# Weight transfers gated behind the first q and k, preparation split, its early squares moved to ScalarE, its steps spread over slots, in a fused attention and feed-forward kernel

## The chip, the cores and the metric

One core of a Trainium2 chip. The metric is device time in microseconds (us). Times of a kernel are the median of its executions; most agree within 1%. A profile is one execution, with positions counted from the start of its span, which is about 2 us shorter than the time that the run reports.

PE is the engine of matmuls, DVE is VectorE, ACT is ScalarE, POOL is GpSimd, SP is the engine that issues the loads of q and k.

## The reference

```python
def _attn_ref(q, k, v, g_q, g_k):          # q, k, v: (8, 12, 448, 64)
    q_n, k_n = rmsnorm(q, g_q), rmsnorm(k, g_k)
    scores = (1 / sqrt(64)) * q_n @ k_n^T
    attn = softmax(scores)
    return attn @ v

x = attn_out as (3584, 768)
out = ((x @ w1) * (x @ w2)) @ w3 @ w_out   # d_ff = 1024
```

## The kernel before

The 96 heads are worked on in 24 "quads" of four heads, three quads to a batch. A quad takes four slots. In each slot PE makes scores for two of the quad's eight score tiles (`sc`), ACT takes their exp into `P`, and PE multiplies the last quad's `P` with v (`pv`). Before that, a quad has to be prepared: squares of q and k, their sums (`ssq`), `alpha` = 1/rms by ln and exp on ACT, scaling on DVE (`qtmp`, `qks`), and a transpose into `qkT`, on PE for quads 0 to 3. As w3 and w_out are constants, their product `w34s` is made once: eight steps "fc" of one transpose of w3 (`w3T`) and two groups of matmuls (`wps`). When a batch is done, its feed-forward pieces (`pa`, `pb`, `po`) become fillers, two to a slot.

Parts that the change and the argument touch (shortened; `...` marks cuts):

```python
def prep_sq(i, pr, on_act=False):
    ...
    for t, src in enumerate((s["q"], s["k"])):
        if on_act:
            nc.scalar.activation(out=sq[:, t], in_=src[:, hs], func=AF.Square)
        else:
            nc.gpsimd.tensor_tensor(out=sq[:, t], in0=src[:, hs], in1=src[:, hs], op=MULT)
    nc.vector.tensor_reduce(out=s["ssq"][:, :, hs, :], in_=sq, axis=AX, op=ADD)

def prep_alpha(i):
    ...
    nc.scalar.activation(out=lnv, in_=s["ssq"], func=AF.Ln, bias=eps_t)
    nc.scalar.activation(out=s["alpha"], in_=lnv, func=AF.Exp, scale=-0.5)

# start
load_qk(0, split=2); load_qk(1); load_qk(2)      # issued by SP
load_v(0); 4 x load_wout; make_identity; 4 x load_w3   # issued by POOL
...
# slots
for i in range(NQ + 1):
    ...                       # preps: quad i+1 (i < 3) and quad i+2 (i >= 2)
    for sl in range(4):
        if i < NQ: qk_exp(i, sl)
        if i > 0 and sl < 3: pv_set(i - 1, sl)
        ...
        for n in preps:
            if sl < 2:
                prep_sq(n, sl)
                if sl == 1: prep_alpha(n)
        ...                   # two weight transfers issued
        ...                   # one fc of w34 from slot 6 on, or two fillers
        for n in preps:
            if sl >= 2:
                prep_scale(n, sl - 2, pe=n < 4)
                if n < 4: prep_pe_transpose(n, sl - 2)
```

Each engine works through its instructions in the order in which they are written here.

## Time and profile before

Time before: 431.25 us (median of 4; 430.7 to 432.7). The profile, by stages: up to the first scores, from there to the first w3 transpose, to the first `pa`, to the end.

The windows view of the kernel before: after the stretch and its length comes each engine's busy time with the number of its instructions, then the granted TensorE clock, the DMA engines' share and GB/s.

```profile
0.00:21.70 21.70, 2.13 (x16) 1.27 (x16) 7.16 (x13) 4.35 (x7) 8.37 (x17) 1.00 0.96 195
21.70:45.90 24.20, 12.87 (x93) 4.75 (x92) 14.69 (x14) 11.69 (x16) 16.72 (x24) 1.00 1.15 242
45.90:99.80 53.90, 42.86 (x357) 22.44 (x354) 35.89 (x57) 18.97 (x30) 19.34 (x22) 0.91 0.49 95
99.80:430.70 330.90, 324.11 (x2552) 148.48 (x2548) 227.50 (x313) 199.19 (x305) 95.79 (x88) 1.00 0.59 120
```

PE is the bound only in the last stretch (324.1 of 330.9 us busy, with the end of the last output in it). The first three stretches are 99.8 us in which PE has 57.9 us of work; the room for a gain lies there.

In the middle, two VectorE multiplies collide with GpSimd squares. The timeline of the kernel before; columns: start, duration, engine, line, operation, out<-in, shapes.

```profile
...
32.79 2.70 DVE L158 TENSOR_TENSOR qtmp<-q_sb,alpha 112x512 bf16<-112x512 f32 x1
...
32.89 1.05 POOL L139 TENSOR_TENSOR sq<-q_sb 112x512 f32<-112x512 f32 x1
33.89 1.04 POOL L139 TENSOR_TENSOR sq<-k_sb 112x512 f32<-112x512 f32 x1
...
35.87 2.85 DVE L171 TENSOR_TENSOR qks<-k_sb,alpha 112x512 bf16<-112x512 f32 x1
...
36.11 1.05 POOL L139 TENSOR_TENSOR sq<-q_sb 112x512 f32<-112x512 f32 x1
37.11 1.04 POOL L139 TENSOR_TENSOR sq<-k_sb 112x512 f32<-112x512 f32 x1
```

The `qtmp` multiply took 2.70 us and the `qks` from `k_sb` 2.85 us, each while two squares ran on GpSimd; undisturbed both take 0.69 us.

### The profile page before, as it was taken

The page shows a single profiled execution, that of the slowest core. Times are in us where ns is not written, and L with a number is a line of the kernel's source. Part 1 is how long each engine was busy: PE and PEld are TensorE (multiplying, and loading weights), DVE is VectorE, ACT ScalarE, POOL GpSimd, SP SyncE. Part 2 cuts the span into 40 slices and gives each one's busy share as a digit, 9 for nine tenths or more (in the row PEclk, how much of TensorE's full clock was granted, in tenths as well). Part 3 has the DMA queues.
Part 4 walks back from the last instruction along what each step waited for, and adds up shares of the span by engine and source line. Part 5 has one row for each costly group of instructions (what it writes and reads, how often), then busy time and mean ns, then how long its engine had stood idle before and what let it go on. Part 6 is the DMA issues. An engine that isn't in the chain of part 4 may idle for free.

```text
span 430.7 us, 7455 instructions
## 1 busy us (share of the span) xinstructions
PE 382.0 (89%) x3008; PEld 176.9 (41%) x3008; DVE 285.2 (66%) x396; ACT 234.2 (54%) x357; POOL 140.2 (33%) x150
## 2 busy tenths in 40 slices
PE   0145688789999999999999999999999999999995
PEld 0111344444444444444444444444444454445552
DVE  1547666676677877977888779777987795233232
ACT  2154344146675766566757665766576657662210
POOL 6177618004412531542355324531452350000000
PEclk9999989889999999999999999999999999999999
DMA  7999944242477579587765677679766764103004
GB/s 148 240 250 234 215 107 66 44 104 47 108 149 145 139 128 139 120 191 151 135 140 152 136 150 143 156 148 143 134 156 129 149 126 111 23 0 111 2 8 138
DMA packets 79362, 55.07 MB, mean 128 GB/s; under 512 B 39904, under 2 KB 73184, under 8 KB 79328
## 3 DMA queue, kind: packets, MB, share of 16 engines
q1 hardware_dynamic: 64160, 42.27, 42.0%
q0 software_dynamic: 15168, 12.32, 20.1%
q8 instruction: 23, 0.38, 0.3%
q14 instruction: 11, 0.09, 0.1%
HBM read 46.72 MB, written 11.01 MB: 134 GB/s over the span
## 4 chain that ended last, share of the span: by engine, by line
PE 81%; DVE 8%; DMA 4%; ACT 2%; issue 1%; POOL 1%; SPq 1%; DVEq 0%
PE pa L279 18%; PE pb L296 17%; PE po L318 16%; PE pv L229 13%; PE sc L205 10%; PE wps L265 5%; DMA k_sb<-in_k_dram 4%; DVE qtmp L158 2%; DVE ssq L142 2%; ACT P L214 2%; DVE qks L171 2%; DVE qks L165 1%; POOL sq L139 1%; SPq L92 1%; PE w3T_ps L257 1%
## 5 line engine op out<-in xcount | busy, mean ns | idle before, releaser
L214 ACT ACTIVATE P<-sc 112x896 bf16<-112x896 f32 x192 | 165.3, 913 | 110.2 <-PE sc L205 110.2
L139 POOL TENSOR_TENSOR sq<-q_sb 112x512 f32<-112x512 f32 x46 | 53.9, 1171 | 192.5 <-DMA q_sb<-in_q_dram 172.9
L279 PE MATMUL pa<-xT,w1s 128*128 128x448 bf16 x384 | 83.7, 354 | 0.0
L296 PE MATMUL pb<-xT,w2s 128*128 128x448 bf16 x384 | 83.1, 353 | 0.0
L303 DVE TENSOR_TENSOR abT<-pb,a_sb 128x448 bf16<-128x448 f32 x64 | 39.7, 621 | 63.5 <-PE pb L296 45.0
L318 PE MATMUL po<-w34s,abT 128*128 128x384 bf16 x448 | 77.1, 327 | 0.5 <-DVE o_sb L325 0.4
L142 DVE TENSOR_REDUCE ssq<-sq 112x16 f32<-112x1024 f32 x48 | 57.9, 1211 | 11.8 <-ACT sq L137 7.5
L205 PE MATMUL sc<-qkT 64*112 64x448 bf16 x384 | 60.6, 388 | 2.8 <-ACT P L214 2.8
L139 POOL TENSOR_TENSOR sq<-k_sb 112x512 f32<-112x512 f32 x46 | 54.5, 1186 | 7.6 <-DMA k_sb<-in_k_dram 7.3
L318 PEld LDWEIGHTS <-abT 128*128 128x128 bf16 x448 | 42.1, 98 | 35.1 <-issue 9.1
L296 PEld LDWEIGHTS <-w2s 128*128 128x128 bf16 x384 | 37.6, 98 | 35.1
L279 PEld LDWEIGHTS <-w1s 128*128 128x128 bf16 x384 | 32.9, 98 | 45.4 <-issue 20.7
L171 DVE TENSOR_TENSOR qks<-k_sb,alpha 112x512 bf16<-112x512 f32 x48 | 49.3, 1027 | 0.0
L287 ACT CAST a_sb<-pa 128x448 bf16<-128x448 f32 x64 | 33.6, 525 | 22.3 <-PE pa L279 22.3
L229 PE MATMUL pv<-P,v_sb 112*32 112x448 bf16 x768 | 45.3, 357 | 0.0
L325 DVE COPY o_sb<-po 128x384 f32<-128x384 f32 x56 | 30.1, 552 | 22.4 <-PE po L318 22.4
L158 DVE TENSOR_TENSOR qtmp<-q_sb,alpha 112x512 bf16<-112x512 f32 x48 | 42.3, 881 | 1.3 <-ACT alpha L149 1.3
L245 DVE TENSOR_TENSOR xT<-pv,r 128x448 bf16<-128x448 f32 x48 | 29.9, 622 | 18.3 <-PE pv L229 17.6
L190 PE MATMUL qkT_ps<-ident,qks 112*128 112x112 bf16 x64 | 7.6, 259 | 37.9 <-DVE qks L165 34.6
L205 PEld LDWEIGHTS <-qkT 64*112 64x112 bf16 x384 | 18.5, 129 | 37.8 <-issue 36.8
L165 DVE TENSOR_TENSOR qks<-qtmp,g_b 112x512 bf16<-112x512 bf16 x48 | 31.9, 665 | 1.6
L265 PE MATMUL wps<-w_outs,w3T 128*128 128x384 bf16 x128 | 25.1, 352 | 2.5 <-DVE w3T L260 2.5
(32 smaller groups left out, 175.0 us busy)
## 6 DMA issues: line engine op xcount, KB each, us to landing
q_sb<-in_q_dram SPq DMA_DIRECT2D x23, 448.0 KB, 5.8
k_sb<-in_k_dram SPq DMA_DIRECT2D x23, 448.0 KB, 6.2
v_sb<-in_v_dram POOLq DMA_DIRECT2D x24, 224.0 KB, 4.5
out_dram<-o_sb SPq DMA_DIRECT2D x8, 336.0 KB, 2.8
out_dram<-o_sb SPq DMA_DIRECT2D x8, 288.0 KB, 4.2
w3s<-in_moe_w_dram POOLq DMA_DIRECT2D x8, 256.0 KB, 11.8
out_dram<-o_sb SPq DMA_DIRECT2D x8, 240.0 KB, 4.4
w_outs<-in_moe_w_out_dram POOLq DMA_DIRECT2D x4, 384.0 KB, 11.8
```

Source lines behind the costliest of these rows:

```text
L139: nc.gpsimd.tensor_tensor(out=sq[:, t], in0=src[:, hs], in1=src[:, hs], op=MULT)
L142: nc.vector.tensor_reduce(out=s["ssq"][:, :, hs, :], in_=sq, axis=AX, op=ADD)
L158: nc.vector.tensor_tensor(out=qtmp.transpose([0, 2, 1, 3]), in0=s["q"][:, hs], in1=alpha[:, 0, hs].unsqueeze(3).broadcast_to([NP, 2, J, D] ...
L171: nc.vector.tensor_tensor(out=qks[:, 1].transpose([0, 2, 1, 3]), in0=s["k"][:, hs], in1=alpha[:, 1, hs].unsqueeze(3).broadcast_to([NP, 2, ...
L205: nc.tensor.matmul(out=sc[:, u, 0:S], lhsT=qkT[u * D : (u + 1) * D, pr, J + jk, :], rhs=qkT[u * D : (u + 1) * D, pr, 0:J, :].rearrange("d ...
L214: nc.scalar.activation(out=P[:, 2 * pr : 2 * pr + 2, jk, :], in_=sc[:, :, 0:S], func=AF.Exp)
L229: nc.tensor.matmul(out=ps[h * HALF : (h + 1) * HALF, :], lhsT=w, rhs=P[:, h, jk, :], start=(jk == 0), stop=(jk == J - 1), tile_position=(0 ...
L265: nc.tensor.matmul(out=ps[:, 0:NH], lhsT=w3T[:, gc, fc * 128 : (fc + 1) * 128], rhs=w_outs[:, gc, nh * NH : (nh + 1) * NH], start=(gc == 0 ...
L279: nc.tensor.matmul(out=ps[:, 0:S], lhsT=w1s[:, c, fi * 128 : (fi + 1) * 128], rhs=xT[b][:, c, :], start=(c == 0), stop=(c == CM - 1),)
L296: nc.tensor.matmul(out=ps[:, 0:S], lhsT=w2s[:, c, fi * 128 : (fi + 1) * 128], rhs=xT[b][:, c, :], start=(c == 0), stop=(c == CM - 1),)
L303: nc.vector.tensor_tensor(out=abT[bp][:, fi, odd * S : (odd + 1) * S], in0=ps[:, 0:S], in1=a_tiles.pop((b, fi)), op=MULT,)
L318: nc.tensor.matmul(out=ps[:, 0:NH], lhsT=abT[bp][:, fi, t * 128 : (t + 1) * 128], rhs=w34s[:, fi, nh * NH : (nh + 1) * NH], start=(fi == 0 ...
```

## The change

Its intent: let the first q and k have the DMA engines for themselves, by a copy on GpSimd that waits for the last k of quad 0 ahead of all weight issues (the "gate"); prepare quad 0 pair by pair; square on ScalarE for quads 0 to 3, so that GpSimd only issues transfers early on; spread the preparation of quads 1 to 4 evenly over slots 0 to 11, and put PE's transposes one slot after their scaling.

```diff
+        make_identity(nc, ident)
+        nc.gpsimd.tensor_copy(out=gate, in_=st[0]["k"][:, HQ - 1, 0, 0:1])
         load_v(0)
         ...
-        prep_sq(0, 0, on_act=True)
-        prep_sq(0, 1, on_act=True)
-        prep_alpha(0)
-        prep_scale(0, 0, pe=True)
-        ...
+        for pr in range(2):
+            prep_sq(0, pr, on_act=True)
+            prep_alpha(0, 2 * pr, 2 * pr + 2)
+            prep_scale(0, pr, pe=True)
+            prep_pe_transpose(0, pr)
 ...
+    def prep_step(step):
+        n, part = divmod(step, 4)
+        if part < 2:
+            prep_sq(n, part, on_act=n < N_PE_T)          # N_PE_T = 4
+            if part == 1:
+                prep_alpha(n)
+        else:
+            prep_scale(n, part - 2, pe=n < N_PE_T)
 ...                                                     # in a slot t:
                 if i < NQ:
                     qk_exp(i, sl)
                 if i > 0 and sl < 3:
                     pv_set(i - 1, sl)
+                for fn in pe_t:                          # transposes of the slot before
+                    fn()
-                for n in preps: ...                      # squares, alpha
-                for _ in range(2):
+                for _ in range(4):
                     if wq:
                         wq.pop(0)()                      # weight transfers
+                if t in W34_SLOTS: ...                   # about one fc a slot, t = 5 to 14
+                elif not w34q:
                     fill(2)
-                for n in preps: ...                      # scaling, transposes
+                goal = 4 + ((t + 1) * 16 + 11) // 12 if t < 12 else 20 + t - 11
+                while steps_done < min(goal, 4 * NQ):
+                    prep_step(steps_done)
+                    ...                                  # transposes go to pe_t
+                    steps_done += 1
```

More of the change, by code (lines that the diff above doesn't have):

```diff
@@ L74 @@
     ones = const.tile([NP, HALF], BF, name="ones")
+    gate = const.tile([NP, 1], FP, name="gate")
     eps_t = const.tile([NP, 1], FP, name="eps_t")
@@ L142, in prep_sq, with prep_alpha @@
         nc.vector.tensor_reduce(out=s["ssq"][:, :, hs, :], in_=sq, axis=AX, op=ADD)
-    def prep_alpha(i):
+    def prep_alpha(i, h0=0, h1=HQ):
         s = st[i]
-        lnv = prep_pool.tile([NP, 2, HQ, J], FP, tag="lnv", name="lnv")
-        nc.scalar.activation(out=lnv, in_=s["ssq"], func=AF.Ln, bias=eps_t)
-        s["alpha"] = prep_pool.tile([NP, 2, HQ, J], FP, tag="alpha", name="alpha")
-        nc.scalar.activation(out=s["alpha"], in_=lnv, func=AF.Exp, scale=-0.5)
+        if h0 == 0:
+            s["lnv"] = prep_pool.tile([NP, 2, HQ, J], FP, tag="lnv", name="lnv")
+            s["alpha"] = prep_pool.tile([NP, 2, HQ, J], FP, tag="alpha", name="alpha")
+        lnv = s["lnv"][:, :, h0:h1]
+        nc.scalar.activation(out=lnv, in_=s["ssq"][:, :, h0:h1], func=AF.Ln, bias=eps_t)
+        nc.scalar.activation(
+            out=s["alpha"][:, :, h0:h1], in_=lnv, func=AF.Exp, scale=-0.5
+        )
     def prep_scale(i, pr, pe=False):
@@ L352, in fill @@
                 fillers.pop(0)()
+    N_PE_T = 4
+    def prep_step(step):
[6 more added lines that the diff above has]
+            prep_scale(n, part - 2, pe=n < N_PE_T)
     with tc.manual_schedule():
@@ L363 @@
             load_wout(c)
-        make_identity(nc, ident)
         for c in range(4):
             load_w3(c)
+        load_v(1)
         nc.vector.memset(eps_t, 64e-6)
@@ L372 @@
         )
-        prep_sq(0, 0, on_act=True)
-        prep_sq(0, 1, on_act=True)
-        prep_alpha(0)
-        prep_scale(0, 0, pe=True)
-        prep_pe_transpose(0, 0)
-        prep_scale(0, 1, pe=True)
-        prep_pe_transpose(0, 1)
+        for pr in range(2):
[3 more added lines that the diff above has]
+            prep_pe_transpose(0, pr)
         wq = [lambda c=c: load_w3(c) for c in range(4, CF)]
+        wq.append(lambda: load_v(2))
         for h in range(HQ):
@@ L387 @@
                     )
-        W34_FROM = (1, 2)
-        fc_next = [0]
+        wq.append(lambda: load_v(3))
+        w34q = [lambda: w3_transpose(0)]
+        for fc in range(CF):
+            if fc + 1 < CF:
+                w34q.append(lambda fc=fc: w3_transpose(fc + 1))
+            for nh in range(2):
+                w34q.append(lambda fc=fc, nh=nh: w34_unit(fc, nh))
+        W34_SLOTS = {5: 4, 6: 3, 7: 3, 8: 3, 9: 3, 10: 3, 11: 2, 12: 2, 13: 2, 14: 2}
+        steps_done = 4
+        pe_t = []
         for i in range(NQ + 1):
@@ L394 @@
                 load_qk(i + 3)
-            preps = []
-            if i < 3:
-                preps.append(i + 1)
-            if 2 <= i and i + 2 < NQ:
-                preps.append(i + 2)
             for sl in range(4):
+                t = 4 * i + sl
                 if i < NQ:
@@ L404 @@
                     pv_set(i - 1, sl)
-                if sl == 0 and i + 1 < NQ:
+                if sl == 0 and 4 <= i + 1 < NQ:
                     load_v(i + 1)
-                for n in preps:
-                    if sl < 2:
-                        prep_sq(n, sl)
-                        if sl == 1:
-                            prep_alpha(n)
-                for _ in range(2):
+                for fn in pe_t:
+                    fn()
+                pe_t = []
+                for _ in range(4):
                     if wq:
                         wq.pop(0)()
-                if (i, sl) >= W34_FROM and fc_next[0] < CF:
-                    fc = fc_next[0]
-                    if fc == 0:
-                        w3_transpose(0)
-                    if fc + 1 < CF:
-                        w3_transpose(fc + 1)
-                    w34_unit(fc, 0)
-                    w34_unit(fc, 1)
-                    fc_next[0] += 1
-                else:
-                    fill(2)
-                for n in preps:
-                    if sl >= 2:
-                        pe = n < 4
-                        prep_scale(n, sl - 2, pe=pe)
-                        if pe:
-                            prep_pe_transpose(n, sl - 2)
+                if t in W34_SLOTS:
+                    for _ in range(W34_SLOTS[t]):
+                        if w34q:
+                            w34q.pop(0)()
+                elif not w34q:
+                    fill(2)
+                goal = 4 + ((t + 1) * 16 + 11) // 12 if t < 12 else 20 + t - 11
+                while steps_done < min(goal, 4 * NQ):
+                    n, part = divmod(steps_done, 4)
+                    prep_step(steps_done)
+                    if part >= 2 and n < N_PE_T:
+                        pe_t.append(lambda n=n, pr=part - 2: prep_pe_transpose(n, pr))
+                    steps_done += 1
         fill(len(fillers))
```

## The prediction

> **What bounds the kernel now.** From 99.86 us on (first pa matmul) PE is the bound: the windows view gives it 313.4 of 315.1 us busy. Before, it is not: empty until 17.5 us, busy 12.9 of 24.2 us from 21.7 to 45.9 us, and 42.9 of 54.0 us from there to 99.9. The prize lies in the first 100 us. Causes, from the chain of waits and the timeline:
>
> 1. The first q and k share the DMA engines with v, w_out and w3. The four first loads (0.9 MB) land at 6.4, 8.5, 11.2 and 13.8 us while 2.4 MB moves; squares and alpha for all four heads precede any scaling; first scores 21.7 us. k of quad 1 lands at 23.7 us.
> 2. GpSimd squares (1.04 us a half, ScalarE 0.63) stand between its weight issues. While they run, two VectorE multiplies take 2.70 and 2.85 us instead of 0.69. The Trainium skill (SBUF — State Buffer, Who interferes with whom) says that a VectorE instruction with two SBUF inputs contends with a GpSimd one that reads SBUF; this trace agrees.
> 3. PE transposes stand right behind their VectorE scaling: PE waits 7.7 us for qks from 40 to 99.8 us. Some w34 groups run cold: 16 wps matmuls take 4.34 us at 81.3 us, 2.76 at 74.9 (granted clock 0.73 for 80 to 90 us). The skill (TensorE: Matmul & The Clock Gate, What's actually happening) blames idleness; the trace shows slow groups behind PE gaps, not the mechanism.
>
> **What the change does.** No PE work is removed. The gate moves weight transfers behind k of quad 0. ScalarE gains 12 squares (7.6 us), GpSimd loses them (12.5 us). The first alpha is split. Transposes go one slot behind their scaling. Preps of quads 1 to 4 spread over 12 slots; w3/w_out work starts one slot earlier at about one fc per slot.
>
> **On the path.** At the 240 GB/s seen with both queues, 1.1 MB alone should be in by about 9 us instead of 13.8; the last half's square, reduce, ln/exp, three multiplies and transposes cost about 5 us (estimate from the durations): first scores near 14.5 us, 7 earlier. k of quad 1 lands about 15 to 17 us. Slots 0 to 4 are then bound by ScalarE (1.7 us of exp a slot plus squares): the first w3 transpose moves from 45.9 to about 29 us. Weights do not decide: 12 MB at 240 GB/s is done by about 55 us, w3's first chunk by about 27. From there to the fillers warm PE work is about 40 us (8 × 3.2 w34, scores 5, pv 7, transposes 3), VectorE work about as much; with a quarter for waits 51 us instead of 54, but one slot further. First pa near 78 us instead of 99.9, with one slot (1.4 us) less left. PE's remaining 313 us and the 16 us end stay. Sum: 431.5 − 22 − 1.4 ≈ 408 us.
>
> **Right or wrong will show as:** k of quad 0 in before 10 us; first scores 13 to 16 us; k of quad 1 before 18 us; no early multiply over 1 us before quad 4; PE waits for qks below 2 us between 40 us and first pa; first pa 72 to 84 us; first pa to end within 3 us of 330.
>
> **What would make it wrong.** ScalarE waiting for alpha inside a slot, holding back exp (in-order queues); VectorE, at about PE's load, stalling PE through the two shared mm buffers; weights arriving late, so w34 or first pa waits for DMA; a low granted clock through the denser stretch. Better than predicted if w34 runs at 3.2 us a slot without waits: near 398 us.
>
> Chances: faster 0.96, within 2% 0.03, slower 0.01. Predicted 408 us, range 398 to 417.

## The result, and the profile after

425.2 us (424.95 to 425.86 in the four fast executions of five), against 431.25 us; the ratio is 0.9857, 95% interval 0.983 to 0.9885. Ratios here and below are the mean time of one kernel's fast runs over that of the other's of the same rounds, so not quite the ratio of the medians. The change gains 6 us where 23 were forecast, and the range 398 to 417 us missed.

The fifth, which came first, took 971.9 us. In it groups of six `pa` matmuls took 3.16 us instead of 1.24 from beginning to end, and PE was 98% busy. It is left out of everything below; what caused it was not found. The change's trace is that of a further execution of the same kernel, run for it:

> The changed kernel, unedited. Its first profile fell in an execution of 972 us in which every matmul was about 2.8 times slower, while four other executions took 425 us. If that execution was an accident of the chip and not of the kernel, this one takes 424 to 427 us, with 128x448 matmuls at 0.19 us apart as in the kernel before, and the profile can be compared. My forecast's mechanism then says first pa at 72 to 84 us and 330 us from there to the end. The rival, since only 6 us were gained: the first pa comes near 93 us because the w34 stretch is slower than 51 us. A second rival: the first pa does come near 78 us and the later stretch is longer by some 15 us.

It took 425.85 us. The windows view of the changed kernel, cut at the same events:

```profile
0.00:16.10 16.10, 2.14 (x16) 1.27 (x16) 6.96 (x13) 4.63 (x9) 6.11 (x15) 1.00 0.88 201
16.10:36.70 20.60, 12.44 (x82) 5.27 (x82) 12.07 (x17) 16.16 (x26) 5.78 (x10) 1.00 1.14 235
36.70:90.00 53.30, 43.11 (x371) 23.14 (x368) 39.67 (x57) 21.26 (x33) 19.79 (x27) 0.94 0.72 134
90.00:423.90 333.90, 327.44 (x2546) 150.81 (x2544) 209.78 (x311) 196.92 (x304) 89.64 (x88) 0.99 0.57 119
```

| stage | before | forecast | after | forecast was off by |
|---|---|---|---|---|
| start to first scores | 21.7 | 14.5 | 16.1 | +1.6 |
| to the first w3 transpose | 24.2 | 14.5 | 20.6 | +6.1 |
| to the first `pa` | 53.9 | 49 | 53.3 | +4.3 |
| to the end | 330.9 | 329.5 | 333.9 | +4.4 |
| span | 430.7 | 407.5 | 423.9 | +16.4 |

(The forecast's stages are differences of the positions it names: 14.5, 29 and 78 us, and the last stretch of before less 1.4 us. Its text names 51 us for the third stretch, which its positions do not bear out.) All four terms were too small, and the last stretch even grew. Three places of the changed kernel's timeline say why. First, slot 1, whose exps come late (columns as before; in brackets the idle time of the engine before the line, and what ended it):

```profile
...
19.57 2.35 DVE L143 TENSOR_REDUCE ssq<-sq 112x16 f32<-112x1024 f32 x2 [2.73 <-ACT sq L138]
19.95 0.63 ACT L138 ACTIVATE sq<-k_sb 112x512 f32<-112x512 f32 x1
...
21.95 0.32 ACT L151 ACTIVATE lnv<-ssq,eps_t 112x32 f32<-112x32 f32 x1 [1.38 <-DVE ssq L143]
22.30 0.23 ACT L152 ACTIVATE alpha<-lnv 112x32 f32<-112x32 f32 x1
22.44 3.33 ACT L219 ACTIVATE P<-sc 112x896 bf16<-112x896 f32 x4
...
23.39 0.62 PE L210 MATMUL sc<-qkT 64*112 64x448 bf16 x2 [4.22 <-ACT P L219]
```

ScalarE has the squares of quad 1, then the ln for its alpha, which waits 1.38 us for the reduce; only then come the exps of slot 1 (22.44), and PE waits 4.22 us for a score buffer before the scores of slot 2.

Second, slot 8, from 52.9 to 64.7 us:

```profile
...
54.19 4.50 DVE L170 TENSOR_TENSOR qks<-qtmp,g_b 112x512 bf16<-112x512 bf16 x1
54.37 1.05 POOL L140 TENSOR_TENSOR sq<-q_sb 112x512 f32<-112x512 f32 x1
...
55.37 1.04 POOL L140 TENSOR_TENSOR sq<-k_sb 112x512 f32<-112x512 f32 x1
...
56.37 1.04 POOL L140 TENSOR_TENSOR sq<-q_sb 112x512 f32<-112x512 f32 x1
57.37 1.03 POOL L140 TENSOR_TENSOR sq<-k_sb 112x512 f32<-112x512 f32 x1
...
58.75 1.16 PE L195 MATMUL qkT_ps<-ident,qks 112*128 112x112 bf16 x8 [4.35 <-DVE qks L170]
```

The collision of before is back at another place: a `qks` multiply that takes 0.42 us elsewhere takes 4.50 us, as long as all four GpSimd squares of quad 4, and PE waits 4.35 us for it. It ended at 58.69, 0.29 us after the last square. The `wps` group behind it, which began at 60.6 us, then takes 4.18 us instead of the 2.76 of slots 6 and 9. Overlap alone does not always do this: from 88 to 92 us in the same trace three multiplies overlapped four squares and took 0.87, 1.15 and 1.52 us, and the last three squares took 1.10 to 1.48 us.

Third, in the last stretch ScalarE waits for reduces. The waits view of ScalarE, first for the kernel before from 99.8 us on, then for the changed one from 90 us on; columns: who waited for whom, us in total, times, longest:

```profile
...
ACT lnv L147 <- DVE ssq L142: 24.2, 18, 2.0
...
```
```profile
...
ACT lnv L151 <- DVE ssq L143: 47.2, 18, 3.8
...
```

How such a wait reaches PE, in the changed kernel's timeline:

```profile
101.75 0.62 DVE L308 TENSOR_TENSOR abT<-pb,a_sb 128x448 bf16<-128x448 f32 x1 [1.48 <-PE pb L301]
...
102.29 1.21 DVE L143 TENSOR_REDUCE ssq<-sq 112x16 f32<-112x1024 f32 x1
...
103.53 0.32 ACT L151 ACTIVATE lnv<-ssq,eps_t 112x32 f32<-112x32 f32 x1 [2.46 <-DVE ssq L143]
...
104.02 1.70 ACT L219 ACTIVATE P<-sc 112x896 bf16<-112x896 f32 x2
...
105.33 0.84 PE L210 MATMUL sc<-qkT 64*112 64x448 bf16 x4
...
```

The reduce stands on VectorE behind `abT` (the product of a feed-forward step), which waits for PE; the ln waits for the reduce, the exps stand behind the ln, and the four score matmuls take 0.84 us instead of 0.59.

### The profile page after: what moved, and what is told of

It is laid out like the page before. It is cut to its first block, busy times and chain, and to the rows that moved or that the text cites. A ratio compares the mean times of both kernels' runs of the same rounds, so it can differ in the third digit from the quotient of the medians.

```text
span 969.9 us, 7465 instructions
## 1 busy us (share of the span) xinstructions
PE 945.7 (98%) x3008; PEld 296.3 (31%) x3008; DVE 253.7 (26%) x396; ACT 247.2 (25%) x371; POOL 115.2 (12%) x139
## 4 chain that ended last, share of the span: by engine, by line
PE 97%; DVE 1%; ACT 1%; DMA 0%; issue 0%; SPq 0%
PE pa L284 21%; PE po L323 21%; PE pb L301 21%; PE pv L234 16%; PE sc L210 10%; PE wps L270 7%; PE w3T_ps L262 1%; PE qkT_ps L195 1%; DVE ssq L143 1%; ACT P L219 1%; DMA k_sb<-in_k_dram 0%; DVE qtmp L163 0%; ACT sq L138 0%; DVE qks L170 0%; ACT lnv L151 0%
## 5 line engine op out<-in xcount | busy, mean ns | idle before, releaser
L301 PE MATMUL pb<-xT,w2s 128*128 128x448 bf16 x384 | 215.6, 758 | 0.0
L284 PE MATMUL pa<-xT,w1s 128*128 128x448 bf16 x384 | 206.0, 737 | 0.0
L323 PE MATMUL po<-w34s,abT 128*128 128x384 bf16 x448 | 201.8, 676 | 0.0
L210 PE MATMUL sc<-qkT 64*112 64x448 bf16 x384 | 111.9, 695 | 4.9 <-ACT P L219 4.7
L323 PEld LDWEIGHTS <-abT 128*128 128x128 bf16 x448 | 72.2, 166 | 130.2 <-issue 128.9
L301 PEld LDWEIGHTS <-w2s 128*128 128x128 bf16 x384 | 67.3, 175 | 132.5 <-issue 132.2
L234 PE MATMUL pv<-P,v_sb 112*32 112x448 bf16 x768 | 104.7, 715 | 0.0
L270 PE MATMUL wps<-w_outs,w3T 128*128 128x384 bf16 x128 | 67.2, 765 | 0.0
L234 PE MATMUL pv<-P,ones 112*32 112x448 bf16 x384 | 52.8, 717 | 0.0
L234 PEld LDWEIGHTS <-v_sb 112*32 112x32 bf16 x768 | 29.4, 135 | 64.0 <-issue 62.2
L140 POOL TENSOR_TENSOR sq<-k_sb 112x512 f32<-112x512 f32 x40 | 41.5, 1038 | 0.0
## 6 DMA issues: line engine op xcount, KB each, us to landing
w3s<-in_moe_w_dram POOLq DMA_DIRECT2D x8, 256.0 KB, 14.8
```

The lines of the kernel that those rows point to most:

```text
L210: nc.tensor.matmul(out=sc[:, u, 0:S], lhsT=qkT[u * D : (u + 1) * D, pr, J + jk, :], rhs=qkT[u * D : (u + 1) * D, pr, 0:J, :].rearrange("d ...
L234: nc.tensor.matmul(out=ps[h * HALF : (h + 1) * HALF, :], lhsT=w, rhs=P[:, h, jk, :], start=(jk == 0), stop=(jk == J - 1), tile_position=(0 ...
L270: nc.tensor.matmul(out=ps[:, 0:NH], lhsT=w3T[:, gc, fc * 128 : (fc + 1) * 128], rhs=w_outs[:, gc, nh * NH : (nh + 1) * NH], start=(gc == 0 ...
L284: nc.tensor.matmul(out=ps[:, 0:S], lhsT=w1s[:, c, fi * 128 : (fi + 1) * 128], rhs=xT[b][:, c, :], start=(c == 0), stop=(c == CM - 1),)
L301: nc.tensor.matmul(out=ps[:, 0:S], lhsT=w2s[:, c, fi * 128 : (fi + 1) * 128], rhs=xT[b][:, c, :], start=(c == 0), stop=(c == CM - 1),)
L323: nc.tensor.matmul(out=ps[:, 0:NH], lhsT=abT[bp][:, fi, t * 128 : (t + 1) * 128], rhs=w34s[:, fi, nh * NH : (nh + 1) * NH], start=(fi == 0 ...
```

## The experiments

Each kernel was timed in three rounds beside the kernel before. The first column of positions is of the first scores, then the first w3 transpose and the first `pa`, then the length from there to the end; all from one profile each.

| kernel | us, median (range) | ratio to before (95%) | scores | w3 | `pa` | to end |
|---|---|---|---|---|---|---|
| before | 431.3 (430.7 to 432.7) | | 21.7 | 45.9 | 99.8 | 330.9 |
| changed | 425.2 (425.0 to 425.9) | 0.986 (0.983 to 0.989) | 16.1 | 36.7 | 90.0 | 333.9 |
| before + gate | 427.3 (424.9 to 428.9) | 0.993 (0.988 to 0.998) | 16.5 | 40.5 | 92.9 | 330.2 |
| changed, no gate | 424.3 (422.3 to 424.5) | 0.984 (0.980 to 0.988) | 17.9 | 41.0 | 88.1 | 332.1 |
| changed, quad 4's squares on ACT | 418.1 (418.1 to 419.9) | 0.971 (0.968 to 0.975) | 16.2 | 36.8 | 83.8 | 332.2 |
| changed, w34s copies on ACT | 416.6 (416.4 to 417.0) | 0.967 (0.964 to 0.970) | 16.3 | 36.9 | 82.3 | 332.1 |
| quad 4's squares on ACT, no gate | 423.1 (421.7 to 425.2) | 0.982 (0.978 to 0.987) | 17.7 | 40.6 | 88.2 | 333.7 |
| quad 4's squares on ACT and again on POOL, unused | 421.3 (418.0 to 425.4) | 0.975 (0.970 to 0.981) | 16.3 | 36.9 | 89.5 | 334.0 |
| both: squares and w34s on ACT | 417.9 (416.7 to 419.4) | 0.970 (0.966 to 0.974) | 16.2 | 36.7 | 82.4 | 332.4 |
| both, and late alpha | 412.9 (412.7 to 413.7) | 0.958 (0.956 to 0.961) | 16.2 | 34.8 | 82.2 | 329.5 |
| changed, late alpha | 415.5 (414.5 to 418.2) | 0.965 (0.960 to 0.969) | 16.1 | 34.8 | 83.7 | 330.0 |
| changed, quads 1 to 3 squared on POOL | 437.1 (436.0 to 441.6) | 1.017 (1.010 to 1.024) | 16.1 | 55.1 | 102.2 | 332.2 |
| changed, transposes at once | 428.6 (425.6 to 430.5) | 0.994 (0.988 to 0.999) | 16.1 | 39.1 | 94.8 | 333.7 |
| squares of quad 4 on ACT, late alpha | 411.3 (410.9 to 412.8) | 0.955 (0.951 to 0.958) | 16.1 | 34.6 | 79.5 | 329.1 |
| the same again ("base") | 411.6 (411.5 to 413.5) | 0.956 (0.952 to 0.959) | 16.1 | 34.6 | 79.6 | 329.7 |
| base, extra matmuls from the start | 416.7 (415.9 to 416.9) | 0.966 (0.963 to 0.969) | 19.9 | 38.0 | 84.1 | 330.1 |
| base, no gate | 417.2 (416.7 to 417.6) | 0.967 (0.964 to 0.970) | 18.7 | 40.1 | 86.0 | 329.3 |
| base, extra matmuls in slots 0 to 4 | 412.1 (410.6 to 412.5) | 0.955 (0.950 to 0.959) | 16.2 | 34.3 | 80.3 | 329.8 |

All outputs are right.

### 1. The gate alone, and all but the gate

```diff
 # the kernel before
+        make_identity(nc, ident)
+        nc.gpsimd.tensor_copy(out=gate, in_=st[0]["k"][:, HQ - 1, 0, 0:1])
         load_v(0)
         ...                      # make_identity stood here
```

> The kernel before, with the gate alone. Theory (the gate pays only together with the squares on ScalarE): the first scores come near 16.5 us instead of 21.7, but GpSimd's second pair of squares of quad 1 still stands behind two gated w3 issues in its order, so that quad 1 is no earlier than before and the time is 429 to 432 us. Rival (the gate is the gain): 425 to 427 us.

427.3 us, between the two expectations and outside both. The first scores came at 16.5 us as expected and slot 3 only 1.2 us earlier than before (30.9 against 32.1), so quad 1 was held up as the theory said. But the two long multiplies of before did not occur: in this trace no early multiply took over 1.1 us. The squares on GpSimd had shifted against the multiplies. Slot 4 began 5.4 us earlier than before (33.9 against 39.3), so 4.2 us of that were won between slots 3 and 4, where the long multiplies of before had stood. So the gain was mostly the missed collision, as far as one profile of the fastest execution tells, and the time scatters by 4 us from run to run.

```diff
 # the changed kernel
-        nc.gpsimd.tensor_copy(out=gate, in_=st[0]["k"][:, HQ - 1, 0, 0:1])
+        nc.gpsimd.memset(gate, 0.0)
```

> The changed kernel without the gate; everything else as changed. Theory: k of quad 1 lands near 23 us again, its square stands on ScalarE ahead of the exps of slot 1 and holds them back by about 5 us; 429 to 432 us. Rival (the gate does nothing): 424 to 427 us.

424.3 us: the rival's number, but not for the rival's reason. The first w3 transpose did come 4.3 us later (41.0 against 36.7), as the theory said. Slot 8 then took 6.4 us instead of 11.8, and no multiply was long before 86 us. The gate's 4 us were there and were lost to the collision, which the kernel without the gate happened to miss. This reading needed a test.

### 2. The collision in slot 8

```diff
-            prep_sq(n, part, on_act=n < N_PE_T)
+            prep_sq(n, part, on_act=n <= N_PE_T)
```

> The changed kernel with the squares of quad 4 on ScalarE too. Theory: the multiply of 4.5 us at 54.2 us, which held PE back by 4.4 us and let it run cold after, was waiting for the four GpSimd squares of quad 4; without them it takes 0.42 us, slot 8 takes about 6 us instead of 11.8, and the time is 419 to 422 us. Rival (PE would have waited for something else there, or ScalarE's added 2.5 us cost as much): 424 to 427 us.

418.1 us. The timeline of this kernel at the same place:

```profile
...
53.64 0.42 DVE L170 TENSOR_TENSOR qks<-qtmp,g_b 112x512 bf16<-112x512 bf16 x1
53.99 0.68 DVE L176 TENSOR_TENSOR qks<-k_sb,alpha 112x512 bf16<-112x512 f32 x1
...
54.12 0.37 PE L195 MATMUL qkT_ps<-ident,qks 112*128 112x112 bf16 x4 [0.27 <-DVE qks L170]
...
54.73 0.37 PE L195 MATMUL qkT_ps<-ident,qks 112*128 112x112 bf16 x4 [0.23 <-DVE qks L176]
```

The multiply takes 0.42 us, PE waits 0.27 us instead of 4.35, and slot 8 takes 6.2 us. First `pa` at 83.8 us instead of 90.0. The theory held and its rival fell.

Is it GpSimd's running, or something that quad 4's data brings? The same squares were put back on GpSimd, into a tile that nothing reads:

```diff
+            if n == N_PE_T:
+                junk = prep_pool.tile([NP, 2, 2, J, D], FP, tag="junk", name="junk")
+                ... nc.gpsimd.tensor_tensor(out=junk[:, u], in0=src[:, hs], in1=src[:, hs], op=MULT)
```

> Squares of quad 4 on ScalarE and used from there, and the same four squares on GpSimd again into a tile that nothing reads. Theory (the VectorE multiply is held by GpSimd running its two-input instructions, whatever they are for): the long multiply near 54 us is back at 3 to 4.5 us, and the time is 422.5 to 426 us. Rival (the wait was one for the data or buffers of quad 4, and goes with the dependence): 417 to 420 us.

```profile
...
53.97 1.05 POOL L369 TENSOR_TENSOR junk<-q_sb 112x512 f32<-112x512 f32 x1
53.98 4.32 DVE L170 TENSOR_TENSOR qks<-qtmp,g_b 112x512 bf16<-112x512 bf16 x1
...
54.98 1.05 POOL L369 TENSOR_TENSOR junk<-k_sb 112x512 f32<-112x512 f32 x1
...
55.97 1.04 POOL L369 TENSOR_TENSOR junk<-q_sb 112x512 f32<-112x512 f32 x1
56.97 1.03 POOL L369 TENSOR_TENSOR junk<-k_sb 112x512 f32<-112x512 f32 x1
```

The long multiply is back (4.32 us), with nothing depending on those squares. The time is 421.3 us, between the two expectations, and the executions spread from 418.0 to 425.4 us, so not each of them collided. This profile fell in the slowest, which by the rule of 1.5% counts as slow; so the timing alone decides nothing here, and the line in the trace is what speaks. With the experiment before it, the cause is shown: the squares on GpSimd hold the multiply, whatever they are for.

```diff
-        nc.vector.tensor_copy(out=w34s[:, fc, ...], in_=ps[:, 0:NH])
+        nc.scalar.copy(out=w34s[:, fc, ...], in_=ps[:, 0:NH])
```

> The changed kernel with the copies of w34s out of PSUM (16 of 0.56 us) on ScalarE instead of VectorE. Theory (in the w34 stretch VectorE's order, where each scaling stands behind a copy that waits for PE, is what PE waits for): the stretch from the first w3 transpose to the first pa shrinks from 53 us by 4 to 8 us; 417 to 422 us. Rival (the stretch is bound by PE itself, cold or not): within 2 us of 53, and 424 to 427 us.

416.6 us, the stretch from the first w3 transpose to the first `pa` 45.4 us instead of 53.3. That is the theory's number. But in this trace the 4.5 us multiply was gone as well (the longest there took 1.23 us), so the gain might have been that. Both edits together tell:

```diff
-            prep_sq(n, part, on_act=n < N_PE_T)
+            prep_sq(n, part, on_act=n <= N_PE_T)
-        nc.vector.tensor_copy(out=w34s[:, fc, ...], in_=ps[:, 0:NH])
+        nc.scalar.copy(out=w34s[:, fc, ...], in_=ps[:, 0:NH])
```

> Squares of quad 4 and the copies of w34s both on ScalarE. The two edits alone gave 418.1 and 416.6, and in both the multiply of 4.5 us was gone. Theory now (both gained mainly by that, and VectorE's order costs only a little beside it): 415 to 417.5 us. Rival (the copies' gain was VectorE's order, and the two add up): 409 to 412 us.

417.9 us (416.7 to 419.4), just above its theory (415 to 417.5). The gains do not add up. In the profiles the stretch from the first w3 transpose to the first `pa` is 45.6 us with both and 47.0 with the squares alone, so VectorE's order behind the copies may cost 1.4 us there, but the time does not show it. Most of the copies' gain alone was that the collision was gone; why it went is argued (they shift VectorE's work), not shown. My theory of the copies fell.

### 3. What the gate is worth

With the squares of quad 4 on ScalarE, as in the first edit of experiment 2, and without the gate:

```diff
-            prep_sq(n, part, on_act=n < N_PE_T)
+            prep_sq(n, part, on_act=n <= N_PE_T)
-        nc.gpsimd.tensor_copy(out=gate, in_=st[0]["k"][:, HQ - 1, 0, 0:1])
+        nc.gpsimd.memset(gate, 0.0)
```

> Squares of quad 4 on ScalarE, and no gate. In the changed kernel taking the gate out cost nothing (424.3 us), although scores of slots 2 to 6 came 3 to 4 us later; slot 8 took 6.4 us there instead of 11.8. Theory (the gate is worth about 4 us, and without it the GpSimd squares of quad 4 happened to miss the multiply): with the squares out of the way in both, no gate costs 3.5 to 5 us against 418.1, so 421.5 to 423 us. Rival (the gate is worth nothing, weights coming later take back what it gives): 417 to 419.5 us.

423.1 us (421.5 to 423 expected) against 418.1 with the gate. It was run at another time. The same edit with its base, the best version (experiment 6):

> The base without the gate. Theory (the gate is worth 4 to 5 us once nothing later eats it): 3 to 5.5 us over the base. Rival: within 1 us of it.

417.2 against 411.6 us (ratios 0.967 and 0.956). The gate is worth 5.6 us when nothing later eats it. With it the last k of quad 0 is in by 8.2 us (when the gate copy starts in the base's trace) instead of 13.9 (when its square starts without the gate), and the w3 transposes begin 5.4 us earlier. The Trainium skill (DMA: Bandwidth & Descriptors, Issuing engines are not separate DMA queues) says that transfers from different issuing engines run on the same 16 DMA engines and interleave; these numbers agree.

### 4. The late alpha

First on the kernel with both edits of experiment 2 (squares of quad 4 and copies of `w34s`):

```diff
         if part < 2:
             prep_sq(n, part, on_act=...)
-            if part == 1:
-                prep_alpha(n)
         else:
+            if part == 2:
+                prep_alpha(n)
             prep_scale(n, part - 2, pe=n < N_PE_T)
```

> As the kernel with both edits, and each alpha one prep step later, so that ScalarE has the exps of the next slot in front of the ln that waits for the reduce. Theory (ScalarE standing still for alpha in slots 1 and 5 holds back exp and so PE; part of what my forecast of slots 0 to 5 missed): slot 2 starts near 19.7 us instead of 23.4, the first w3 transpose 1 to 3 us earlier, and the time falls by 1 to 3 us against the kernel with both edits. Rival (quad 1 and 2 are bound by their prep chain, not by the exps): within 0.7 us of it.

412.9 against 417.9 us: a gain of 5 us where 1 to 3 were expected. The first w3 transpose comes 1.9 us earlier; slot 2 started at 21.5, not 19.7. The larger part was not expected: from the first `pa` to the end it takes 329.5 us instead of 332.4. The same diff alone on the changed kernel:

> The changed kernel with each alpha one prep step later and nothing else. Theory (from the four edits so far: 1.9 us of the late alpha's gain lay in slots 0 to 5, 2.9 us after the first pa, where ScalarE no longer stands behind a reduce that stands behind abT): first pa to the end falls from 333.8 to 329 to 331 us, and the time by 3 to 6 us, to 419.5 to 422.5, with the long multiply of slot 8 still there. Rival (the late alpha gains only beside the other two edits): 424 to 427 us.

415.5 us, more than expected, and 330.0 us from the first `pa` to the end against 333.9. Its waits view of ScalarE in that stretch has no wait of `lnv` any more:

```profile
ACT P L219 <- PE sc L210: 77.6, 78, 2.4
ACT a_sb L292 <- PE pa L284: 33.5, 36, 4.4
ACT lns L244 <- PE pv L234: 2.1, 1, 2.1
```

So what the late alpha undoes is shown: the 47.2 us of waits (24.2 before) are gone, and of the 78 score groups of four in the stretch none takes 0.84 us any more, where in the changed kernel seven did (1.8 us in all; none in the kernel before). That those waits came of moving all preparation behind the fillers is read from the order of the code and the chain above. A second piece of the 333.9 us is another thing: the first `pa` and `pb` groups took 1.67 and 2.45 us instead of 1.31 and 1.30, 1.5 us more. Kernels that kept the early alpha but began the stretch at the usual pace took 332.1 to 332.4 us (slow beginners 333.7 to 334.0); why some begin it slowly was not taken apart. The rest of the gain of this kernel is again the collision, shorter here: one multiply of 2.40 us at 57.8 us.

### 5. The change's other parts, undone one at a time

```diff
-            prep_sq(n, part, on_act=n < N_PE_T)
+            prep_sq(n, part)                          # quads 1 to 3 on GpSimd
```

> The changed kernel with the squares of quads 1 to 3 back on GpSimd. Theory (GpSimd's squares stand behind weight issues that wait for landings, so quad 1 is late again, and multiplies collide with squares again): slot 4 starts near 33 us instead of 28.5, and the time is 428 to 433 us. Rival (ScalarE gains nothing by being taken): 423 to 427 us.

437.1 us, worse than the kernel before and beyond the expectation. Slot 4 started at 41.5 us where 33 was expected; the expected collisions were not there (no multiply over 1 us before 101 us). The timeline shows the chain:

```profile
27.70 0.53 POOL L118 DMA_DIRECT2D w3s<-in_moe_w_dram  x1 [2.25 <-DMA w_outs<-in_moe_w_out_dram]
29.00 0.53 POOL L118 DMA_DIRECT2D w3s<-in_moe_w_dram  x1 [0.77 <-DMA w3s<-in_moe_w_dram]
29.55 1.05 POOL L140 TENSOR_TENSOR sq<-q_sb 112x512 f32<-112x512 f32 x1
...
34.87 0.32 ACT L151 ACTIVATE lnv<-ssq,eps_t 112x32 f32<-112x32 f32 x1 [16.43 <-DVE ssq L143]
...
36.31 0.62 PE L210 MATMUL sc<-qkT 64*112 64x448 bf16 x2 [17.19 <-ACT P L219]
```

GpSimd's first squares of quad 1 began at 29.5 us, behind w3 issues that each wait for an earlier transfer to land; the ln on ScalarE waited 16.43 us for them, and the scores of slot 2 waited 17.19 us for the exps of slot 1. In this order of issue the change is a loss without the squares on ScalarE; whether the gate does the harm there was not run apart.

```diff
-                        pe_t.append(lambda n=n, pr=part - 2: prep_pe_transpose(n, pr))
+                        prep_pe_transpose(n, part - 2)
```

> The changed kernel with PE's transposes straight behind their scaling, not one slot later. Theory: each of the five or six halves that fall into the w34 stretch makes PE wait about 1.7 us for qks, as before the change; time 429 to 434 us. Rival (in the changed kernel the scaling stands behind a copy that waits for PE, so the delay of one slot hides little): 423 to 427 us.

428.6 us (425.6 to 430.5), 3.4 us over the changed kernel, just under the expectation. It was run at another time. PE waits for `qks` in three waits of up to 2.5 us, 5.9 us in all between 36 and 100 us, though the collision was small in this profile (one multiply of 1.48 us). The delay of one slot is worth something, of the order of 3 us, with a scatter as large.

### 6. Both remedies, and what is left

The squares of quad 4 on ScalarE and the late alpha, without the copies:

```diff
-            prep_sq(n, part, on_act=n < N_PE_T)
-            if part == 1:
-                prep_alpha(n)
+            prep_sq(n, part, on_act=n <= N_PE_T)
         else:
+            if part == 2:
+                prep_alpha(n)
```

> Squares of quad 4 on ScalarE and the late alpha, without the copies of w34s on ScalarE, which gave nothing beside the squares. Theory: the two gains add, 411.5 to 414.5 us, as with all three edits (412.9). Rival (the copies were needed for the late alpha's gain): 416 to 419 us.

411.3 us, just under the expectation: the late alpha gains 6.8 us on top of the squares, and the copies of `w34s` were not needed. Singly the two edits had gained 7.2 and 9.8 us on the changed kernel, together 13.9, since the late alpha alone had met a shorter collision already. This version beats both kernels. What remained was my forecast of slots 0 to 4, where PE runs at a slow pace; did that pace cost?

```diff
+        ...                          # wz: a constant tile
+        def keep_warm(n):
+            ps = mm_psum.tile([128, 512], FP, tag="mm", name="warm")
+            for _ in range(n):
+                nc.tensor.matmul(out=ps, lhsT=ident, rhs=wz, start=True, stop=True)
+        keep_warm(28)                # before the first prep
 ...
                     qk_exp(i, sl)
+                if t < 5:
+                    keep_warm(4)
```

> The kernel with the squares of quad 4 on ScalarE and the late alpha, again, as the base of the two others: 410.5 to 413 us.

> The base, with 28 matmuls of a constant into a tile that nothing reads before the first prep, and 4 more in each of slots 0 to 4. Theory (my forecast of slots 0 to 5 took PE's later durations; there PE runs at half pace, score groups 0.99 instead of 0.59 us, pv 1.69 instead of 0.94): kept busy, PE does them in the later time, the first w3 transpose comes 1.5 to 3 us before the base's 34.6, and the time is 1.5 to 3 us under the base. Rival (these slots are bound by the exps and the prep chain, PE's pace is hidden, or the extra matmuls cost what they give): within 1 us of the base or over it.

The base took 411.6 us. The run with extra matmuls took 416.7 and was confounded: the 28 began at 6.2 us, behind the write of their operand, and ended at 14.8, so the first scores came 3.8 us late. Without them:

```diff
-        keep_warm(28)
```

> The base (squares of quad 4 on ScalarE, late alpha; 411.6 us, ratio 0.9555) with four extra matmuls in each of slots 0 to 4 and none before. The run with 28 of them ahead of the first prep was spoiled: they began at 6.2 us, behind the write of their operand, and still ran when the first transposes were ready, which came 4.4 us late. From the first scores to the first w3 transpose it took 18.1 us against the base's 18.5, though PE ran at its later pace from slot 2 on. Theory left (PE's pace is hidden there, ScalarE is the bound, busy 15.9 of 18.5 us): 18 to 19 us again, and the time within 1.5 us of the base. Rival (PE's slow pace costs): the stretch is 16.5 us or less, and the time 1.5 to 3 us under the base.

412.1 us (410.6 to 412.5), no change. The timelines of PE in slots 3 and 4, base first, then with the extra matmuls:

```profile
...
23.92 1.16 PE L195 MATMUL qkT_ps<-ident,qks 112*128 112x112 bf16 x8 [1.03 <-DVE qks L170]
...
25.00 0.99 PE L210 MATMUL sc<-qkT 64*112 64x448 bf16 x4
...
27.94 0.99 PE L210 MATMUL sc<-qkT 64*112 64x448 bf16 x4
```
```profile
...
23.95 0.37 PE L195 MATMUL qkT_ps<-ident,qks 112*128 112x112 bf16 x4 [0.29 <-DVE qks L170]
...
24.85 0.59 PE L210 MATMUL sc<-qkT 64*112 64x448 bf16 x4
...
25.37 1.04 PE L394 MATMUL warm<-wz,ident 128*128 128x512 bf16 x4
...
27.60 0.59 PE L210 MATMUL sc<-qkT 64*112 64x448 bf16 x4
```

There the score groups took 0.59 instead of 0.99 us, yet the stretch from first scores to first w3 transpose took 18.1 us against 18.5. PE's pace is hidden there but for 0.4 us at most; the rival fell. ScalarE is busy for 15.9 of the base's 18.5 us in that stretch:

```profile
...
16.10:34.60 18.50, 11.84 (x82) 4.55 (x81) 11.76 (x17) 15.93 (x26) 4.65 (x8) 1.00 1.15 234
...
```

## Why the prediction was wrong

The time was forecast as 408 us (398 to 417) and is 425.2. The direction was right; the size was four times too large. The base with its two small edits, at 411.6 us, lies in the forecast's range, but by luck: its stretches are 16.1, 18.5, 44.9 and 329.7 us where 14.5, 14.5, 49 and 329.5 were forecast, so errors of 1.6 and 4.0 us in the first two cancel one of 4.1 in the third.

- **"First scores near 14.5 us": 16.1.** The last k came as forecast (8.9 us), but the reduce of the second pair stood on VectorE behind the first pair's transposed copy and began at 12.0 us, 1.9 us after its squares. The pair-wise split has this price: with the gate and without the split the first scores came at 16.5 us (experiment 1), so it gave 0.4 us. Off by 1.6 us.
- **"Slots 0 to 4 are then bound by ScalarE (1.7 us of exp a slot plus squares): ... about 29 us": 36.7.** The bound fits what was seen (ScalarE busy 15.9 of 18.5 us once the alpha is late; speeding PE up gave nothing), though no run lightened ScalarE. The term was mis-sized: 20.6 us instead of 14.5. ScalarE's own work in the stretch is 16.2 us, 2.2 of it the ln and exp for alpha and for the softmax's division (`lns`, `r`), which the forecast's bracket does not name. Its ln waited 2.9 us more for reduces, of which the late alpha wins back 1.9 (20.6 against 18.7 with it alone). I had named "ScalarE waiting for alpha inside a slot" as a thing that could go wrong and put nothing for it into the sum. PE's slow pace, the other candidate, costs 0.4 us at most.
- **"With a quarter for waits 51 us": 53.3.** Its mechanism failed. Taking the squares of quads 1 to 3 off GpSimd did not end the collisions: I expected "no early multiply over 1 us before quad 4", but GpSimd, in step with no slot of PE, ran ahead to quad 4's squares (written in slot 9, run in PE's slot 8) while quad 3 was being scaled, and one multiply took 4.5 us. Without that the stretch takes 47.0 us (experiment 2), and with the late alpha too 45.0, so less than forecast. The wait of PE for `qks` from 40 us to the first `pa` was 5.5 us, 4.35 of it this one, where I forecast less than 2. This is the step of the forecast that failed outright: at about 7 us in time (425.2 against 418.1) it is the largest single loss.
- **"PE's remaining 313 us and the 16 us end stay": 333.9 instead of 329.5.** Wrong: the diff moved alpha behind the fillers of every slot to the end of the kernel, and I read it for the first 15 slots only. Seven late score groups are 1.8 us of the excess, the slow first `pa` and `pb` 1.5; neither is there with the late alpha (330.0).
- **"Weights do not decide"** held: no w34 or `pa` matmul waited for a weight. And **the gate** does about what was forecast: it is worth 5.6 us, where 7 were named for it and the split together.

Left open: the 972 us execution; why the collisions come in some executions only (the spread of the run with unused squares), and why the overlap at 88 to 92 us held the multiplies so much less; why the last stretch begins slowly in some profiles; and how much of the delayed transposes' 3 us is scatter.

## What to carry to other kernels

Two engines that block each other make a gain elsewhere a lottery: shift one by a few us and a collision appears or goes, so look in the trace for single instructions far above their usual duration before crediting a change with what the clock says. An instruction that waits for another engine belongs in its queue behind the work that is ready, not ahead of it, in every slot where the pattern repeats and not only in the start-up that the change is about. When undoing a part seems to cost nothing, look at whether the stage it serves lost its time and a later one won it back.

## What the Trainium skill lacked or had wrong

- SBUF — State Buffer, Who interferes with whom: it says that a VectorE instruction with two SBUF inputs contends with a GpSimd instruction that reads SBUF, and that the order of issue decides who blocks. The runs agree with the first. On the second they leave doubt: by the profile the multiply of slot 8 began 0.18 us before the first square and was still the one held (starts on GpSimd are rough, so the order is not certain). The page does not tell what happens against several such instructions in a row: here a multiply of 0.42 us took 4.50 us, until all four squares were done.
- TensorE: Matmul & The Clock Gate, What's actually happening: it tells of PE at a slow pace when little used, which agrees with score groups of 0.99 us in slots 3 and 4 and 0.59 once extra matmuls kept it busy. The granted clock in the profile read 1.00 in that very stretch, which agrees with the page's warning (Seeing it yourself) not to trust clock events fully; here the durations of like matmuls told the pace.
- The section Seeing it yourself tells of a clock stuck low for over 50 us. One execution here had six `pa` matmuls in 3.16 us instead of 1.24 for all of its 970 us, at a granted clock noted as 1.0; the passage speaks of no whole execution, and the cause is not known here.
